# One-hot rows and columns of a token router, built for five token tiles by one comparison each, and their matmuls placed earlier

## The chip, the core and the metric

The kernel runs on one core of a Trainium2 chip. The metric is the device time of one execution in microseconds (us). Engines are named as in the profile: PE is TensorE (matmuls), PEld its weight loads, DVE is VectorE, ACT is ScalarE, POOL is GpSimd and SP is SyncE. Each engine works through a queue of its own in program order. What one engine hands to another is guarded by semaphores.

## The reference, cut to what matters

Attention through 32 packed vectors for each head (4 batches, 8 heads, 576 tokens), a mixture of 8 experts with the best two for each of the 2304 tokens, and a gated feed-forward layer:

```
p_packed = sm_attn(p, k, v);  x = sm_attn(q, p_packed, p_packed)
noisy = x @ w_gate + log1p(exp(x @ w_noise)) * noise
top2 of noisy for each token, weights by softmax over the two
out[token] += weight * (relu(x @ w1[e]) @ w2[e])      # for its two experts e
y = (silu(x @ w_gate2) * (x @ w_val)) @ w_out
```

The change is in the routing between the first two stages. Each pair (token, choice) gets a slot: expert number times 18 tiles of 128 rows, plus its rank in that expert. For the gathers of the experts' rows the kernel needs the inverse table `idx[row, column]`, which says what token sits in each slot. It is made by matmuls of one-hot matrices. For a tile of 128 tokens and choice k, `ohr[token, r] = (slot & 127 == r)` is 128 wide and `ohc[token, c] = (slot >> 7 == c)` is 144 wide (`NCOL`). The product of `ohr` transposed with `ohc` times the token number adds each token number into its place.

## The kernel before, in words

The whole program is one list of steps in the order in which it is issued. For attention, routing and the first two expert blocks that order stands in a string, `PLAN`, which is run step by step. `s1.t.h`, `mx`, `ex`, `et`, `eo`, `av`, `pp`, `pt`, `po`, `gp`, `s2`, `sa` to `sc`, `op` and `oo` are the steps of attention for group t of eight (scores, maximum, exponentials, transposes and so on). `u.i.f` is an up-projection of expert block i (12 matmuls 256 wide, written below as u), `h.i.f` splits its result into a high part `hh` (ACT, L664) and a low part `hl` (DVE, L665), and `d.i.f` is the down-projection (6 matmuls 512 wide). `g.i` gathers and transposes an expert block's rows (PE L610, then ACT L611 `xTh`, DVE L612 `xTl`). `L` turns the loader of expert weights: ACT makes the high part of a piece (L148), POOL or DVE the low part (L149).

`r.j` takes one step of the routing generator `route(j, ...)`. Router 0 and router 1 have five token tiles each and run inside attention; router 2 has ten tiles and runs beside the up- and down-projections of the first expert block. A step ends at each `yield`. Five tiles make a group; router 2 has two groups. A group's twelve steps are, before the change: ten steps of one pair (tile, choice) each, with two comparisons on DVE (L561 `ohr`, L563 `ohc`) and a scaling by the token number on ACT (L565 `ohv`); an eleventh with ten matmuls into one PSUM bank (L570); a twelfth in which DVE adds that bank to `idxf` (L573, at the end L579 into `idx`). Buffers: ten of `ohr`, three of `ohc`, ten of `ohv`.

The plan's steps around router 2's two groups, with the group's steps written as A1 to A12 and B1 to B12, stand so:

```
h.0.5 A1 A2 A3 d.0.4 A4 A5 A6 u.0.7 A7 A8 xo.7 d.0.5 A9 A10 h.0.6 g.1 A11
h.0.7 L A12 B1 B2 B3 B4 d.0.6 B5 u.1.0 B6 B7 B8 d.0.7 S u.1.1 B9 h.1.0 u.1.2
B10 u.1.3 B11 h.1.1 B12 d.1.0 (tail)
```

Router 0's group in the plan, cut: `oo.3.1`, steps 1 and 2, `s2.4.1`, steps 3 and 4, `mx.6.0 ... lg.1`, then `pp.5`, step 5, `pt.5`, step 6, `s1.6.1` (whose maximum is `mx.6.1`), step 7, and so on to step 12.

Of the kernel before, what the change touches and what calls it, by code (L numbers as in the profile page):

```python
# [14 lines left out]
F16 = mybir.dt.float16  # L15
I32 = mybir.dt.int32
U32 = mybir.dt.uint32
AF = mybir.ActivationFunctionType
ALU = mybir.AluOpType
# [10 lines left out]
NCOL = E * COLS  # L30
# [69 lines left out]
def body(ctx, tc, qT, kT, v, pT, noise, wgn, w1, w2, wx, out):  # L100
    nc = tc.nc
    ve = nc.vector
# [29 lines left out]
    def bank():  # L132
        return psum.tile([128, 512], F32, name="bank", tag="bank")
# [52 lines left out]
    ap2 = att.enter_context(tc.tile_pool(name="ap2", bufs=2, side="right"))  # L186
# [37 lines left out]
    def iota(name, shape, pattern, base=0, mult=0, dt=F32):  # L224
        t = ap1.tile(shape, dt, name=name)
        nc.gpsimd.iota(t, pattern=pattern, base=base, channel_multiplier=mult,
                       allow_small_or_imprecise_dtypes=True)
        return t
# [3 lines left out]
    io128 = iota("io128", [128, 128], [[1, 128]], dt=F16)  # L232
    io144 = iota("io144", [128, NCOL], [[1, NCOL]], dt=F16)
    tokid = iota("tokid", [128, NT], [[S, 4], [128, 5]], base=-MID, mult=1)
# [172 lines left out]
    def route(j, b0, b1):  # L407
        nt = 5 * (b1 - b0)
        t0 = 5 * b0
        l = lg[:, t0:t0 + nt, :]  # L410

        def tmp(name, dt=F32, shape=(128, nt, 8)):
            return ap1.tile(list(shape), dt, name=f"{name}_{j}")
        z = l[:, :, 8:16]
        nzb, fn, r, p, rz, u, den, s, w = (tmp(n) for n in ("nzb", "fn", "r", "p", "rz", "u", "den", "s", "w"))
# [104 lines left out]
        for c in range(nt):  # L520
            nc.tensor.matmul(rk[:, c + 1:], ones, mm[:, c:c + 1, :].to_broadcast([128, nt - c, 8]),
                             start=False, stop=c == nt - 1, skip_group_check=True)
# [20 lines left out]
        if b1 <= 2:  # L543
            s0 = tmp("s0", shape=(128, 2, 3))
            ve.scalar_tensor_tensor(s0, ixf[:, :, 0:3], float(FIRST - COLS * 128), sf[:, :, 0:3],
                                    op0=ALU.mult, op1=ALU.add)
# [6 lines left out]
        rf = tmp("rf", shape=(128, 2, 2, nt))  # L553
        ve.tensor_copy(rf, ri)
        yield
        for g in range(0, nt, 5):
            oh_ = []
            for c in range(g, g + 5):
                for k in range(2):
                    ohr = ap2.tile([128, 128], F16, name="ohr", bufs=10)  # L560
                    ve.tensor_scalar(ohr, io128, rf[:, 0, k, c:c + 1], None, op0=ALU.is_equal)  # L561
                    ohc = ap2.tile([128, NCOL], F16, name="ohc", bufs=3)
                    ve.tensor_scalar(ohc, io144, rf[:, 1, k, c:c + 1], None, op0=ALU.is_equal)  # L563
                    ohv = ap2.tile([128, NCOL], F16, name="ohv", bufs=10)
                    nc.scalar.activation(ohv, ohc, AF.Copy, scale=tokid[:, t0 + c:t0 + c + 1])  # L565
                    oh_.append((ohr, ohv))
                    yield
            pt = bank()[:, :NCOL]
            for n, (ohr, ohv) in enumerate(oh_):
                nc.tensor.matmul(pt, ohr, ohv, start=n == 0, stop=n == 9)  # L570
            yield
            if t0 + g + 5 < NT:
                ve.tensor_tensor(idxf, idxf, pt, op=ALU.add)  # L573
                if t0 + g + 5 == NT // 2:
                    for e in range(2):
                        ve.tensor_scalar(idx0[:, 2 * e:2 * e + 2], idxf[:, COLS * e:COLS * e + 2], float(2 * S - 1), None,
                                         op0=ALU.min)
            else:
                ve.tensor_tensor(idx, idxf, pt, op=ALU.add)  # L579
            yield  # L580
# [129 lines left out]

    loader = Loader([(*x[:3], engs[c]) for c, x in zip(ENG["lo"], [x for e in range(2) for x in expert_pieces(e, (ve, ve))])])
    jobs = [route(j, *x) for j, x in enumerate(JOBS)]
    blk_ = EARLY + [(0, 2, 3)]
    preps, UP, HID = {}, {}, {}
# [22 lines left out]
    def dn(i, f):  # L737
        down(*down_expert(blk_[i], f, HID.pop((i, f))))
    do = dict(wg=lambda: nc.sync.dma_start(wg, wgn), nz=lambda: nc.sync.dma_start(nz, noise), xo=store_x, lk=load_k, lv=load_v, lq=load_q, s1=s1, mx=max1, ex=exp1, et=e1t, eo=e1t_out, rc=rec1, av=av1, pp=pp,
              pt=ppt, po=ppt_out, gp=gproj, go=gproj_out, s2=s2, sa=s2a, se=s2e, sb=s2b, sc=s2c, op=oproj, oo=oout,  # L740
# [3 lines left out]
    for x in PLAN.split():  # L744
        x, _, n = x.partition("*")
# [416 lines left out]
    for i, blk in enumerate(blocks):  # L1162
        e, t0, nt = blk
# [191 lines left out]
```

## Time and profile before

| | |
|---|---|
| median of 3 runs | 1037.73 us (1034.54 to 1038.38) |
| profiled execution | 1037.31 us, span from first to last instruction 1035.5 us |
| mean granted clock of TensorE | 0.982 of full speed |
| PE busy | 978.0 us (94% of the span) |
| PEld, DVE, ACT, POOL busy | 864.9, 678.6, 421.5, 355.5 us |
| routing's comparisons on DVE (L561, L563) | 12.8 and 12.1 us, 40 instructions each, between 54.6 and 144 us |
| routing's ten-matmul groups on PE | four, ending at 73.4, 91.2, 133.2 and 144.7 us |

The profile is that of one execution. The 1.8 us between its time and its span lie around the program. A busy share is an average: DVE is busy for two thirds of the span as a whole, but almost without a gap in the attention and routing stage, which ends near 145 us; after it PE is busy nearly all the time.

### The profile page before, as it was taken

How to read it: one execution, taken by the hardware profiler on the slowest of the kernel's cores; microseconds unless marked ns; L12 is line 12 of the kernel's file. 1: busy time of each engine (PE TensorE's matmuls, PEld its weight loads, DVE VectorE, ACT ScalarE, POOL GpSimd, SP SyncE). 2: the span in 40 equal slices, each digit the busy share in tenths (PEclk: the TensorE clock that was granted, in tenths of full speed). 3: DMA queues.
4: the chain of work that ended last, by engine and by line, in shares of the span. 5: the costliest groups of instructions: out<-in, count | busy, mean ns of one | idle time of the engine just before them, and what ended most of it. 6: DMA issues, size and time to landing. Idle time of an engine off the chain costs nothing.

```text
span 1035.5 us, 15235 instructions
## 1 busy us (share of the span) xinstructions
PE 978.0 (94%) x5415; PEld 864.9 (84%) x5415; DVE 678.6 (66%) x1536; ACT 421.5 (41%) x859; POOL 355.5 (34%) x409
## 2 busy tenths in 40 slices
PE   6967799989999899998999999999999999999996
PEld 3534689979888798998988898999999999999995
DVE  5998973466565646555645475678865678756764
ACT  2665253465455545555544434222423224132220
POOL 1333532344643545445454414321232211111100
PEclk9978999999999999999999999999999999999999
DMA  8934543377675767666764679887798768777741
GB/s 288 299 122 146 170 136 116 126 273 269 212 264 191 270 204 251 229 202 245 246 225 159 194 210 311 238 236 214 217 303 235 230 184 255 234 199 222 216 147 65
DMA packets 99045, 221.41 MB, mean 214 GB/s; under 512 B 8080, under 2 KB 37392, under 8 KB 96656
## 3 DMA queue, kind: packets, MB, share of 16 engines
q0 software_dynamic: 46752, 104.87, 34.9%
q1 hardware_dynamic: 47024, 101.32, 28.9%
q10 hardware_dynamic: 5184, 14.16, 3.6%
q8 instruction: 45, 0.74, 0.3%
q14 instruction: 40, 0.33, 0.1%
HBM read 172.08 MB, written 48.23 MB: 213 GB/s over the span
## 4 chain that ended last, share of the span: by engine, by line
PE 74%; DVE 10%; DMA 5%; POOL 3%; issue 3%; ACT 3%; SPq 0%; ACTq 0%; POOLq 0%; DVEq 0%
PE bank L628 23%; PE bank L630 23%; PE bank L629 23%; DMA row<-x_dram,idx 3%; POOL sums L801 1%; DMA stg<-in_w 1%; PE bank L610 1%; PE bank L388 1%; POOL w L149 1%; DVE p L460 1%; DVE sums L824 1%; PE bank L919 1%; ACT w L148 1%; POOL sums L795 1%; DMA kt<-in_kT 1%
## 5 line engine op out<-in xcount | busy, mean ns | idle before, releaser
L628 PE MATMUL bank<-w 128*128 128x384 f32 x504 | 170.4, 338 | 0.6 <-ACT hh L993 0.5
L630 PE MATMUL bank<-w 128*128 128x384 f32 x504 | 168.7, 335 | 0.0
L629 PE MATMUL bank<-w 128*128 128x384 f32 x504 | 168.6, 334 | 0.0
L628 PE MATMUL bank<-xTh,w 128*128 128x256 f32 (+1 forms) x512 | 163.1, 319 | 2.8 <-DVE mt L787 2.8
L630 PE MATMUL bank<-xTh,w 128*128 128x256 f32 (+1 forms) x512 | 159.9, 312 | 0.0
L629 PE MATMUL bank<-xTl,w 128*128 128x256 f32 (+1 forms) x512 | 159.7, 312 | 0.0
L665 DVE SCALAR_TENSOR_TENSOR hl<-bank,hh 128x384 fp32r<-128x384 f32 (+1 forms) x128 | 62.4, 488 | 132.3 <-ACT hh L664 125.8
L871 POOL DMA_DIRECT2D w<-wq x72 | 54.4, 756 | 266.3 <-PE bank L630 266.3
L628 PE MATMUL bank<-w,hh 128*128 128x512 f32 x320 | 127.0, 397 | 6.1 <-ACT hh L664 6.1
L630 PE MATMUL bank<-w,hl 128*128 128x512 f32 x320 | 127.4, 398 | 2.8 <-DVE hl L665 2.8
L629 PE MATMUL bank<-w,hh 128*128 128x512 f32 x320 | 127.1, 397 | 0.0
L795 POOL TENSOR_TENSOR sums<-mt,ex 128x256 f32<-128x256 f32 x72 | 54.4, 755 | 170.4 <-DVE mt L787 163.8
L149 POOL TENSOR_TENSOR w<-stg,w 128x1024 fp32r<-128x1024 f32 x37 | 91.4, 2475 | 62.3 <-ACT w L148 62.0
L628 PEld LDWEIGHTS bank<-xTh,w 128*128 128x128 f32 x512 | 98.2, 192 | 7.8 <-DVE mt L787 3.5
L629 PEld LDWEIGHTS bank<-xTl,w 128*128 128x128 f32 x512 | 98.3, 192 | 3.5
L664 ACT ACTIVATE hh<-bank 128x384 fp32r<-128x384 f32 (+1 forms) x128 | 55.5, 433 | 111.5 <-PE bank L630 103.1
L630 PEld LDWEIGHTS bank<-xTh,w 128*128 128x128 f32 x512 | 98.2, 192 | 0.0
L628 PEld LDWEIGHTS bank<-w 128*128 128x128 f32 x504 | 94.6, 188 | 3.1 <-ACT hh L993 1.1
L629 PEld LDWEIGHTS bank<-w 128*128 128x128 f32 x504 | 94.7, 188 | 0.7
L630 PEld LDWEIGHTS bank<-w 128*128 128x128 f32 x504 | 94.6, 188 | 0.0
L630 PE MATMUL bank<-w,lg 128*128 128x512 f32 x204 | 79.7, 391 | 0.0
L629 PE MATMUL bank<-w,hg 128*128 128x512 f32 x204 | 79.7, 390 | 0.0
(222 smaller groups left out, 1838.4 us busy)
## 6 DMA issues: line engine op xcount, KB each, us to landing
w<-wq POOLq DMA_DIRECT2D x36, 1024.0 KB
stg<-in_w SPq DMA_DIRECT2D x64, 512.0 KB
w<-wq POOLq DMA_DIRECT2D x36, 768.0 KB
wd<-in_wx SPq DMA_DIRECT2D x72, 256.0 KB
w<-wxo POOLq DMA_DIRECT2D x18, 1024.0 KB
wq<-his ACTq DMA_DIRECT2D x24, 448.0 KB
wq<-sums SPq DMA_DIRECT2D x24, 448.0 KB
y_dram<-row SPq DMA_DIRECT2D x40, 256.0 KB
```

The lines of the kernel that those rows point to most:

```text
L148: nc.scalar.copy(hi, st)
L149: lo_eng.tensor_tensor(lo, st, hi.bitcast(F32), op=ALU.subtract)
L388: nc.tensor.matmul(PS["o", t, c][:n, :272], E2T[t][:, c * 128:c * 128 + n], PP[t], start=True, stop=True)
L460: el.scalar_tensor_tensor(p, p, c[k], x, op0=ALU.add, op1=ALU.mult)
L610: nc.tensor.transpose(ps[:, k, :n], src[:n, k * 128:(k + 1) * 128], ident[:n, :n])
L628: nc.tensor.matmul(ps, lh, rh, start=start, stop=False, skip_group_check=skip)
L629: nc.tensor.matmul(ps, lh, rl, start=False, stop=False, skip_group_check=skip)
L630: nc.tensor.matmul(ps, ll, rh, start=False, stop=stop, skip_group_check=skip)
L664: nc.scalar.activation(hh[:, :n], ps[:, :n], AF.Relu)
L665: ve.scalar_tensor_tensor(hl[:, :n], ps[:, :n], 0.0, hh[:, :n].bitcast(F32), op0=ALU.max, op1=ALU.subtract)
L795: nc.gpsimd.tensor_tensor(o, mf.rearrange("p (f n) -> p f n", f=2), ex.bitcast(F32).rearrange("p (f n) -> p f n", f=2), op=ALU.mult)
L871: nc.gpsimd.dma_start(w[:, :4 * m].rearrange("p (x n) -> p x n", x=4), src.rearrange("p h k n -> p (h k) n"))
```

## The change

Each group makes all ten `ohr` by one two-operand comparison (10 x 128 columns) and all ten `ohc` by another (10 x 144), with the iota row and the slot numbers both read through broadcast patterns. The iota rows are float16, the slot numbers float32. ACT scales `ohc` in place, once for each token tile (288 columns) instead of once for each pair. The first comparison is step 1 of the group, the second comparison and all five scalings are step 2, three steps are empty, the ten matmuls stand in step 6 (before: step 11), five steps are empty, and the addition stays in step 12. Both tiles have one buffer.

```diff
         for g in range(0, nt, 5):
-            oh_ = []
-            for c in range(g, g + 5):
-                for k in range(2):
-                    ohr = ap2.tile([128, 128], F16, name="ohr", bufs=10)
-                    ve.tensor_scalar(ohr, io128, rf[:, 0, k, c:c + 1], None, op0=ALU.is_equal)
-                    ohc = ap2.tile([128, NCOL], F16, name="ohc", bufs=3)
-                    ve.tensor_scalar(ohc, io144, rf[:, 1, k, c:c + 1], None, op0=ALU.is_equal)
-                    ohv = ap2.tile([128, NCOL], F16, name="ohv", bufs=10)
-                    nc.scalar.activation(ohv, ohc, AF.Copy, scale=tokid[:, t0 + c:t0 + c + 1])
-                    oh_.append((ohr, ohv))
-                    yield
+            ohr = ap2.tile([128, 5, 2, 128], F16, name="ohr", bufs=1)
+            ohc = ap2.tile([128, 5, 2, NCOL], F16, name="ohc", bufs=1)
+            at = [rf[:, x, :, g:g + 5].rearrange("p k c -> p c k").unsqueeze(3) for x in range(2)]
+            ve.tensor_tensor(ohr, io128[:, None, None, :].to_broadcast([128, 5, 2, 128]),
+                             at[0].to_broadcast([128, 5, 2, 128]), op=ALU.is_equal)
+            yield
+            ve.tensor_tensor(ohc, io144[:, None, None, :].to_broadcast([128, 5, 2, NCOL]),
+                             at[1].to_broadcast([128, 5, 2, NCOL]), op=ALU.is_equal)
+            for c in range(5):
+                nc.scalar.activation(ohc[:, c], ohc[:, c], AF.Copy, scale=tokid[:, t0 + g + c:t0 + g + c + 1])
+            yield
+            for _ in range(3):
+                yield
             pt = bank()[:, :NCOL]
-            for n, (ohr, ohv) in enumerate(oh_):
-                nc.tensor.matmul(pt, ohr, ohv, start=n == 0, stop=n == 9)
-            yield
+            for n in range(10):
+                nc.tensor.matmul(pt, ohr[:, n // 2, n % 2], ohc[:, n // 2, n % 2], start=n == 0, stop=n == 9)
+            for _ in range(6):
+                yield
             if t0 + g + 5 < NT:
                 ve.tensor_tensor(idxf, idxf, pt, op=ALU.add)
```

## Rows read from the trace of the kernel before

**Rows 1.** Windows: length, busy of PE, PEld, DVE, ACT, POOL; PE clock; DMA.

```profile
60.00:80.00 20.00, 13.54 (x77) 7.68 (x76) 19.25 (x76) 10.81 (x31) 8.12 (x5) 0.67 0.32 109
...
120.00:130.00 10.00, 6.97 (x44) 6.21 (x43) 9.77 (x44) 3.65 (x7) 4.66 (x2) 0.83 0.44 142
130.00:140.00 10.00, 10.00 (x73) 9.07 (x72) 9.20 (x36) 7.37 (x22) 2.40 (x1) 1.00 0.07 25
```

**Rows 2.** Waits of PE from 124 to 215 us: total, times, longest.

```profile
PE bank L519 <- DVE mm L516: 3.0, 1, 3.0
PE bank L570 <- ACT ohv L565: 2.0, 1, 2.0
```

**Rows 3.** Timeline of PE, router 2: start, duration, line, out<-in, [idle before <-releaser].

```profile
129.21 0.28 PE L628 MATMUL bank<-xTh,w 128*128 128x256 f32 x1
...
132.46 0.79 PE L570 MATMUL bank<-ohv,ohr 128*128 128x144 f16 x10
133.09 0.50 PE L628 MATMUL bank<-w,hh 128*128 128x512 f32 x1
...
136.01 0.40 PE L628 MATMUL bank<-w,hh 128*128 128x512 f32 x1
...
141.71 0.74 PE L570 MATMUL bank<-ohv,ohr 128*128 128x144 f16 x9
144.45 0.22 PE L570 MATMUL bank<-ohv,ohr 128*128 128x144 f16 x1 [2.00 <-ACT ohv L565]
```

**Rows 4.** Timeline of DVE in router 2, first and last of twenty comparisons, and what follows.

```profile
128.94 0.24 DVE L561 TENSOR_SCALAR ohr<-io,rf 128x128 f16<-128x128 f16 x1
...
132.06 0.26 DVE L563 TENSOR_SCALAR ohc<-io,rf 128x144 f16<-128x144 f16 x1
...
133.55 0.69 DVE L612 TENSOR_TENSOR xTl<-bank,xTh 128x512 fp32r<-128x512 f32 x1
134.16 0.41 DVE L665 SCALAR_TENSOR_TENSOR hl<-bank,hh 128x256 fp32r<-128x256 f32 x1
134.49 0.29 DVE L573 TENSOR_TENSOR idxf<-idxf,bank 128x144 f32<-128x144 f32 x1
...
134.86 2.41 DVE L563 TENSOR_SCALAR ohc<-io,rf 128x144 f16<-128x144 f16 x1
...
142.29 1.50 DVE L561 TENSOR_SCALAR ohr<-io,rf 128x128 f16<-128x128 f16 x1
```

**Rows 5.** Timeline of DVE: two-operand instructions from and to SBUF, two sizes.

```profile
103.24 1.20 DVE L149 TENSOR_TENSOR w<-stg,w 128x1024 fp32r<-128x1024 f32 x1
...
121.88 0.33 DVE L511 TENSOR_TENSOR oh<-io,expf 128x160 f32<-128x160 f32 x1
```

**Rows 6.** Timeline of ACT: four scalings, and SBUF-to-SBUF instructions of two widths.

```profile
55.04 1.40 ACT L565 ACTIVATE ohv<-ohc,tokid 128x144 f16<-128x144 f16 x4 [1.90 <-DVE ohc L563]
...
68.68 0.68 ACT L364 ACTIVATE s2a<-s2a 128x576 f32<-128x576 f32 x1 [1.22 <-POOL s2a L357]
...
94.44 0.44 ACT L364 ACTIVATE s2a<-s2a 128x288 f32<-128x288 f32 x1 [1.14 <-DVE s2a L357]
```

**Rows 7.** Timeline of POOL: a weight piece's low part.

```profile
134.81 2.40 POOL L149 TENSOR_TENSOR w<-stg,w 128x1024 fp32r<-128x1024 f32 x1 [8.06 <-ACT w L148]
```

**Rows 8.** Windows of one us after PE's stall that ends at 144.45.

```profile
145.00:146.00 1.00, 1.00 (x4) 0.73 (x3) 0.93 (x6) 0.00 (x0) 0.39 (x1) 0.50 0.95 373
...
148.00:149.00 1.00, 1.00 (x5) 0.80 (x4) 0.89 (x4) 0.24 (x2) 0.87 (x1) 0.82 0.77 209
```

**Rows 9.** Timelines of DVE and PE around router 0's group.

```profile
54.62 0.21 DVE L561 TENSOR_SCALAR ohr<-io,rf 128x128 f16<-128x128 f16 x1
...
57.84 0.33 PE L321 MATMUL bank<-ident,pp 128*128 128x128 f32 x1 [2.31 <-ACT pp L310]
...
60.98 0.45 DVE L269 TENSOR_REDUCE m<-bank 128x1 f32<-128x288 f32 x1
```

**Rows 10.** Waits of PE from 150 us to the end, the largest.

```profile
PE bank L610 <- DMA row<-x_dram,idx: 8.3, 4, 2.8
```

## The prediction

> **What bounds the kernel now.** I read the clock and the span first (one core, granted clock 0.982), then the windows. They show two regimes. Inside attention DVE is the full engine: from 60 to 80 us it is busy 19.25 of 20 us and PE only 13.5 [rows 1]. Beside the first expert block both are full: from 120 to 130 us DVE has 9.77 of 10, and from 130 to 140 PE has all 10 [rows 1]. In the second regime any wait of PE is paid in full by everything behind it. PE's waits from 124 us on are two: 3.0 us for DVE's `mm`, ahead of the one-hots and not touched here, and 2.0 us for the last scaling of router 2's second group [rows 2]. PE takes its instructions in order: nine of the ten matmuls ran at 141.71, the tenth at 144.45, and the down-projection behind it stood still [rows 3]. The last comparison but one had taken 1.50 us in place of 0.24 [rows 4]. After the wait the granted clock is 0.50, the lower of the two levels (1.2 GHz), in the window from 145 us and the two behind it, and 0.82 in the window from 148 [rows 8]: 3.0 + 0.36 us at half speed, so 1.7 us lost. The first group's matmuls, at 132.46, wait for nothing [rows 3].
>
> **What the edit costs on DVE and ACT.** Twenty comparisons of a group start from 128.94 to 132.06 without a gap, 3.12 / 19 = 0.164 us apart, so a group costs 3.28 us of DVE [rows 4]. One instruction on many columns is not in the trace. Two-operand instructions from SBUF take 0.33 us for 160 columns and 1.20 for 1024 [rows 5]: (1.20 - 0.33) / 864 = 1.01 ns a column. That gives 0.33 + 1120 x 1.01 ns = 1.46 us for 1280 columns and 1.62 us for 1440. A comparison lasts 0.24 but the next starts 0.16 after it, so consecutive ones overlap by 0.08: the pair ends 3.00 us after its start. DVE thus saves only 0.28 us a group, 1.1 in all four. Four scalings of 144 columns take 1.40 us, 0.35 each [rows 6]; 288 columns more cost 0.68 - 0.44 = 0.24 us, so 144 more cost 0.12, and one of 288 costs 0.47, five of them 2.35 us [rows 6]. ACT had room (7.37 of 10 us at its fullest here [rows 1]). What matters is that scaling, formerly running beside the comparisons, can now start only when the second big comparison is done: from the group's first comparison to its last scaled column 3.00 + 0.04 + 2.35 = 5.39 us, in place of 132.06 + 0.26 + 0.04 + 0.35 - 128.94 = 3.77 [rows 4, 6].
>
> [...]
>
> **What the move costs: router 2, first group.** The ten matmuls move from step 11 to step 6. In the plan's order, behind the group's first comparison PE has only `d.0.4` ahead of step 6, and it is through with it at 129.21, where `u.0.7` now starts [rows 3]. DVE starts the group at 128.94 [rows 4], ends at 131.94, and ACT at 131.98 + 2.35 = 134.33. PE would stand from 129.21 to 134.33: **5.1 us** of a stall that is not there today, since `u.0.7`, `d.0.5` and `g.1` (129.21 to 132.46, 3.25 us [rows 3]) were its cover and now queue behind it. The clock falls as after the 2.0 us wait: **1.7 us** more (0 to 1.7).
>
> **Second group.** DVE can't run ahead, because ahead of B1 it has the low part of `g.1`'s rows, and those wait for transposes that PE now does 3.25 us after the first group's matmuls. From the transposes' end: ACT's high part and hand-over about 0.65; then by the starts in [rows 4] 0.61 to `hl`, 0.33 to the addition, 0.21 to the first comparison (0.37 to the second one, less a pitch); then 5.39. Sum 7.2 us. PE has `d.0.6` and `u.1.0` meanwhile, 133.09 to 136.01, 2.92 us [rows 3]. The stall is 4.3 us. Between the two comparisons POOL wants its weight piece: ACT's cast of it follows `h.0.7`, so it comes while the first big comparison runs. Today that piece started at 134.81 and lasted 2.40 [rows 7], and the comparison that started behind it took 2.41 in place of 0.25 [rows 4]: DVE's SBUF comparisons and POOL's subtraction exclude each other, and POOL got in between two of them. Taken so again, +2.3: **6.6 us**; without, 4.3. Clock again **1.7**.
>
> **What goes away.** The 2.0 us wait and its 1.7 us of clock: d.1.0 has no matmuls of the router ahead of it. That is the change's gain, **3.7 us**.
>
> **Attention.** Router 0: ACT's first four scalings began at 55.04 and took 1.40, to 56.44 [rows 6]; now five end at 54.62 + 5.39 = 60.0. ACT's `pp.5` behind them, for which PE already waits 2.31 us at 57.84 [rows 9], comes 3.5 us later, then PE's transposes, the ten matmuls (0.6) and the scores whose maximum DVE took at 60.98 [rows 9]. By then DVE has work for part of it only; I put it 2.7 us late, and six later comparisons that are gone (1.0) give some back: +1.7. Bounds: -1 (DVE's saved instructions alone) and +3 (nothing given back). Router 1: its DVE has idle time at PE, so -0.2. I take **+1.5**. An extra PSUM bank held from step 6 to 12 I cost at nothing: the buffers are eight and few are live in router 2's stretch; if a bank is late, the like of it is the 2.0 us wait [rows 2], inside the range. Reading the bank, 0.29 us, is hidden as before [rows 4].
>
> **Sum.** 5.1 + 1.7 + 6.6 + 1.7 - 3.7 + 1.5 = 12.9 us. The later stages are bound by PE with buffers and gathers released by the program's own progress, so the delay passes on. The profiled execution took 1037.31 us (span 1035.5 and 1.8 around it), 0.4 below the median of the three runs: 1037.3 + 12.9 = **1050.2 us**.
>
> **Rivals.** Half a per cent (5.2 us) is about what a measurement of this kernel can tell from no change.
> *Two stalls, POOL not between* (0.22): if POOL's piece comes after both comparisons, -2.3: 1047.9. For it: the piece waits for a cast on ACT; against: 134.81 [rows 7].
> *Two columns a cycle* (0.05): the comparisons at half the price, 1.37 us less a group: stalls of 3.7 and 2.9 + 2.3, router 0 near +0.3; 3.7 + 1.7 + 5.2 + 1.7 - 3.7 + 0.3 = 8.9, 1046.2. Against it speaks [rows 5], one column in 1.01 ns. [...]
> *Absorbed later* (0.14): PE waits 8.3 us for gathered rows after 150 us, in four places [rows 10]. Were these DMAs on a clock of their own, a late PE would find them ready: 12.9 - 8.3 = 4.6, 1041.9, no measurable change. Against: POOL issues them behind its own work, which moves along.
> *Not slower* (0.09): PE reaches both sets of matmuls after the scaled columns, and the 3.7 us with DVE's 1.1 are pure gain: 1032.5. That needs DVE to begin the first group 5.1 us and the second 4.3 us earlier against PE than above. For it: DVE lost time at POOL's pieces shortly before, as in [rows 4]; against: PE waits on the same DVE queue just before, 3.0 us for `mm` [rows 2], so an earlier DVE makes PE earlier too.
>
> **Chances and range.** The forecast with both stalls and POOL between has 0.50, with its own range 1046.5 to 1053.5. Slower by over 0.5% takes the first three and a little of the fourth, 0.80; within, most of the last two, 0.16; faster, the not-slower case with more saved in attention, 0.04. Low bounds of the terms (stall 3.7, second 4.3, clock 0 and 1.7, attention -1) give 3.7 + 4.3 + 1.7 - 3.7 - 1 = 5.0 us, high ones (attention +3) 14.4; the range 1041 to 1053.5 leaves out about two in ten.
>
> **What would show it.** PE's waits: L570 on ACT's scaling twice in router 2, near 5 and 4 to 7 us, each followed by a granted clock of 0.50 for about 3 us; no wait at `d.1.0`; L561 at 1.46 and L563 at 1.62 us, or more beside POOL; ACT's scalings near 0.5. Wrong would be the forecast if the first group's wait were under 2 us, if DVE's timeline put B1 ahead of `g.1`'s rows, or if PE's waits after 150 us shrank by as much as the stalls add.

## The result, and the profile after

The changed kernel takes 1048.36 us (median of 6 runs, 1047.6 to 1052.54) against 1037.84 for the kernel before (6 runs, 1034.54 to 1042.45): a ratio of 1.0111, 95% interval 1.0081 to 1.0142. Its profiled execution took 1047.82 us, with a span of 1045.9 and a mean granted clock of 0.976. In this listing the lines behind the edit stand three lower than before: L572 is the router's ten matmuls, L631 to L633 the up- and down-projections, L566 the scaling.

The waits of PE between 124 and 215 us (waited for: total, times, longest) answer to [rows 2]:

```profile
PE bank L572 <- ACT ohc L566: 8.1, 2, 4.7
PE bank L519 <- DVE mm L516: 3.0, 1, 3.0
```

One wait of 2.0 us has become two that sum to 8.1, both for the scaled columns. PE's timeline shows where, and answers to [rows 3]:

```profile
130.68 0.40 PE L633 MATMUL bank<-w,hl 128*128 128x512 f32 x1
134.45 2.05 PE L572 MATMUL bank<-ohc,ohr 128*128 128x144 f16 x10 [3.37 <-ACT ohc L566]
136.25 0.56 PE L631 MATMUL bank<-xTh,w 128*128 128x256 f32 x1
...
143.95 0.28 PE L633 MATMUL bank<-xTh,w 128*128 128x256 f32 x1
148.94 2.10 PE L572 MATMUL bank<-ohc,ohr 128*128 128x144 f16 x10 [4.71 <-ACT ohc L566]
150.78 0.77 PE L631 MATMUL bank<-w,hh 128*128 128x512 f32 x1
...
157.72 0.40 PE L631 MATMUL bank<-w,hh 128*128 128x512 f32 x1
```

The wait in brackets is not the whole stall: the ten matmuls then come in pairs, each pair behind its own scaling, so that they spread over 2.05 us where they took 0.79 [rows 3]. From the end of `d.0.4` (131.08) to `u.0.7` (136.25) PE loses 5.17 us less the 0.65 of the matmuls themselves, 4.5; from the end of `u.1.0` (144.23) to `d.0.7` (150.78) 6.55 - 0.65 = 5.9. The last row is where `d.1.0` now runs with no wait ahead of it.

The producers, on DVE's timeline, answer to [rows 4]:

```profile
130.78 1.48 DVE L560 TENSOR_TENSOR ohr<-io,rf 128x1280 f16<-128x1280 f16 x1
132.18 1.65 DVE L563 TENSOR_TENSOR ohc<-io,rf 128x1440 f16<-128x1440 f16 x1
...
141.91 0.69 DVE L615 TENSOR_TENSOR xTl<-bank,xTh 128x512 fp32r<-128x512 f32 x1 [5.09 <-ACT xTh L614]
...
143.06 1.49 DVE L560 TENSOR_TENSOR ohr<-io,rf 128x1280 f16<-128x1280 f16 x1
144.47 3.80 DVE L563 TENSOR_TENSOR ohc<-io,rf 128x1440 f16<-128x1440 f16 x1
```

DVE, full before, now stands 5.09 us behind the transposes that PE does late: the first stall delays the second group. POOL's timeline has the piece that came between the two comparisons of that group, and ACT's has five scalings each of router 0's group and of router 2's second; they answer to [rows 7] and [rows 6]:

```profile
143.18 3.57 POOL L149 TENSOR_TENSOR w<-stg,w 128x1024 fp32r<-128x1024 f32 x1 [14.58 <-ACT w L148]
```

```profile
55.85 2.23 ACT L566 ACTIVATE ohc<-ohc,tokid 128x288 f16<-128x288 f16 x5 [4.35 <-DVE ohc L563]
57.99 0.92 ACT L253 COPY xs<-bank 128x272 f32<-128x272 f32 x3
58.81 1.27 ACT L310 ACTIVATE pp<-bank,sum 32x64 f32<-32x64 f32 x4
...
148.36 2.23 ACT L566 ACTIVATE ohc<-ohc,tokid 128x288 f16<-128x288 f16 x5 [5.26 <-DVE ohc L563]
```

The windows of one us behind both stalls (length, busy of PE, PEld, DVE, ACT, POOL, the granted clock, DMA) answer to [rows 8]. The clock is at the lower of the two levels that the trace shows, 0.50 of full speed, from near 136.2 to 139.6, and again from near 146.5, inside the second stall, to 153.3. At 0.50 a projection of 512 columns starts every 0.427 us (151.36 to 152.64, three of them), 1.20 columns a ns, which the forecast writes as 1.2 GHz; at 1.00 one starts every 0.230 us (139.74 to 140.43). The windows left out have 0.50 at 138 and from 147 to 151, and 1.00 from 140 to 146. Projections run through the last 2.5 us of the second stretch, from 150.78 on:

```profile
136.00:137.00 1.00, 0.86 (x6) 0.85 (x5) 0.42 (x1) 0.37 (x2) 0.00 (x0) 0.62 0.00 0
137.00:138.00 1.00, 1.00 (x7) 1.00 (x6) 0.00 (x0) 0.00 (x0) 0.00 (x0) 0.50 0.00 0
...
139.00:140.00 1.00, 1.00 (x5) 0.82 (x5) 0.00 (x0) 0.00 (x0) 0.00 (x0) 0.68 0.00 0
...
151.00:152.00 1.00, 1.00 (x4) 0.81 (x4) 0.00 (x0) 0.00 (x0) 0.00 (x0) 0.50 0.00 0
152.00:153.00 1.00, 1.00 (x3) 0.78 (x3) 0.55 (x1) 0.00 (x0) 0.00 (x0) 0.50 0.07 16
153.00:154.00 1.00, 1.00 (x7) 0.90 (x6) 0.14 (x1) 0.39 (x2) 0.00 (x0) 0.85 0.02 6
```

Around router 0 PE's timeline and DVE's answer to [rows 9]:

```profile
59.49 0.47 PE L321 MATMUL bank<-ident,pp 128*128 128x128 f32 x1 [5.78 <-ACT pp L310]
60.40 1.41 PE L572 MATMUL bank<-ohc,ohr 128*128 128x144 f16 x10
```

```profile
52.80 1.45 DVE L560 TENSOR_TENSOR ohr<-io,rf 128x1280 f16<-128x1280 f16 x1
...
58.95 0.24 DVE L403 TENSOR_TENSOR lg<-xs,xs 128x80 f32<-128x80 f32 x1 [1.22 <-ACT xs L253]
...
63.02 0.46 DVE L269 TENSOR_REDUCE m<-bank 128x1 f32<-128x288 f32 x1 [2.29 <-PE bank L263]
```

To see where the time went I cut each profiled execution at the same instructions: router 0's first comparison (A), its addition to `idxf` (B), router 1's addition (C), router 2's `mm` on DVE, L516 (D), the transposes of twelve rows on PE in `g.2` (E), and the end. In us:

| | start to A | A to B | B to C | C to D | D to E | E to end | span |
|---|---|---|---|---|---|---|---|
| before | 54.6 | 21.4 | 15.7 | 30.6 | 30.8 | 882.4 | 1035.5 |
| after | 52.8 | 24.7 | 15.4 | 31.2 | 40.7 | 881.1 | 1045.9 |
| difference | -1.8 | +3.4 | -0.3 | +0.6 | +9.9 | -1.3 | +10.4 |

Router 2's stretch (D to E) carries nearly all of it. The first column lies ahead of the first instruction that the change touches, and the last one scatters: in the eight kernels below it is 881.6 to 885.2.

### The profile page after: what moved, and what is told of

Its sections match the earlier page's. It is cut to its first block, busy times and chain, and to the rows that moved or that the text cites. A ratio compares the mean times of both kernels' runs of the same rounds, so it can differ in the third digit from the quotient of the medians.

```text
span 1045.9 us, 15139 instructions
## 1 busy us (share of the span) xinstructions
PE 982.2 (94%) x5415; PEld 868.2 (83%) x5415; DVE 675.3 (65%) x1464; ACT 417.0 (40%) x839; POOL 355.2 (34%) x409
## 4 chain that ended last, share of the span: by engine, by line
PE 71%; DVE 10%; DMA 6%; POOL 4%; ACT 4%; issue 3%; ACTq 0%; SPq 0%; POOLq 0%; DVEq 0%
PE bank L631 22%; PE bank L633 22%; PE bank L632 22%; DMA row<-x_dram,idx 3%; POOL sums L804 2%; DMA kt<-in_kT 1%; PE bank L613 1%; POOL w L149 1%; PE bank L388 1%; DMA stg<-in_w 1%; PE bank L263 1%; POOL sums L798 1%; DMA out<-row 1%; PE bank L922 1%; DVE sums L827 1%
## 5 line engine op out<-in xcount | busy, mean ns | idle before, releaser
L631 PE MATMUL bank<-w 128*128 128x384 f32 x504 | 170.8, 339 | 0.4 <-ACT hh L996 0.2
L633 PE MATMUL bank<-w 128*128 128x384 f32 x504 | 169.0, 335 | 0.0
L631 PE MATMUL bank<-xTh,w 128*128 128x256 f32 (+1 forms) x512 | 163.6, 320 | 2.8 <-DVE mt L790 2.8
L633 PE MATMUL bank<-xTh,w 128*128 128x256 f32 (+1 forms) x512 | 160.2, 313 | 0.0
L631 PE MATMUL bank<-w,hh 128*128 128x512 f32 x320 | 127.3, 398 | 5.7 <-ACT hh L667 5.7
L633 PE MATMUL bank<-w,hl 128*128 128x512 f32 x320 | 127.2, 398 | 2.1 <-DVE hl L668 2.0
L631 PEld LDWEIGHTS bank<-xTh,w 128*128 128x128 f32 x512 | 98.5, 192 | 7.6 <-DVE mt L790 3.4
L633 PEld LDWEIGHTS bank<-xTh,w 128*128 128x128 f32 x512 | 98.4, 192 | 0.0
L631 PEld LDWEIGHTS bank<-w 128*128 128x128 f32 x504 | 94.7, 188 | 3.1 <-ACT hh L996 1.0
L633 PEld LDWEIGHTS bank<-w 128*128 128x128 f32 x504 | 94.7, 188 | 0.0
L633 PE MATMUL bank<-w,lg 128*128 128x512 f32 x204 | 79.8, 391 | 0.0
```

The lines of the kernel that those rows point to most:

```text
L631: nc.tensor.matmul(ps, lh, rh, start=start, stop=False, skip_group_check=skip)
L633: nc.tensor.matmul(ps, ll, rh, start=False, stop=stop, skip_group_check=skip)
```

## Experiments

All eight kernels compute the whole reference. Their spans are cut as above; what is timed is given as a ratio to the kernel before, run beside them.

One thing differs among them ahead of the one-hots. In the kernel before, the change, "POOL's piece later", "columns first" with the matmuls in step 11 and the 16-bit kernel, POOL's weight piece runs beside `mm` of router 2, and PE waits 3.0 us for `mm`. In the other five `mm` is short and the piece holds the next large DVE instruction, L531 (2.5 us in place of 0.33); that wait is gone, and the one-hots come later against PE. DVE's timeline, kernel before and two pairs a step:

```profile
122.24 2.30 DVE L516 TENSOR_TENSOR mm<-oh 128x80 bf16<-128x80 f32 x1
```

```profile
120.54 0.24 DVE L516 TENSOR_TENSOR mm<-oh 128x80 bf16<-128x80 f32 x1
```

So a first group's wait can be compared only within one of these two sets; D to E holds the delay in either form. Why the piece falls differently was not traced.

**Matmuls back in step 11.** This keeps the big comparisons and lumped scalings and undoes the move alone.

```diff
-            for _ in range(3):
+            for _ in range(8):
                 yield
...
-            for _ in range(6):
-                yield
+            yield
```

> Big comparisons and scalings as in the changed kernel, but the ten matmuls back at step 11. Order theory (PE stands at matmuls placed ahead of their operands): in router 2's first group PE reaches them at the place of 132.46 while the scaling ends 5.3 us after the first comparison starts, so a wait of 1.8 us is left there (with up to 1.7 us of clock); none in the second group, and the old 2.0 us wait with its 1.7 us of clock is gone; attention costs 2 us more than before, since ACT's five scalings still stand ahead of pp.5. Sum near +1: 1036 to 1041 us. Rival, the batch theory (the big comparisons and lumped scalings cost the time wherever the matmuls stand): within 3 us of the changed kernel, 1045 to 1050.

Measured: 1042.56 us (10 runs), ratio 1.0047 (1.003 to 1.0064). PE's timeline of this kernel:

```profile
134.08 1.99 PE L572 MATMUL bank<-ohc,ohr 128*128 128x144 f16 x10 [1.88 <-ACT ohc L566]
...
144.67 0.92 PE L572 MATMUL bank<-ohc,ohr 128*128 128x144 f16 x10
146.79 0.50 PE L630 MATMUL bank<-w,hh 128*128 128x512 f32 x1 [1.20 <-ACT hh L666]
```

More than half of the loss goes with the move: D to E falls from 40.7 to 32.9. The second group waits for nothing at its matmuls. The time lies between the two expected ranges, above 1041 and below 1045, so the order alone does not explain all of it. As expected, the first group waits 1.88 us, and A to B is still 2.0 us longer than before, with five scalings in a block ahead of ACT's work for attention. Not expected: PE waits for ACT's `hh` behind the router's block, 3.0 us in two places. The granted clock did not fall here: it is 1.00 in every window of four us from 127 to 159. E to the end is 2.8 us longer than before, within the scatter of that column.

**Single comparisons, matmuls early.** The reverse: the code of before with two pairs a step, so that its matmuls too stand in step 6.

```diff
                     oh_.append((ohr, ohv))
-                    yield
+                yield
...
-            yield
+            for _ in range(6):
+                yield
```

> Single comparisons and scalings as in the kernel before, two pairs a step in steps 1 to 5, and the matmuls at step 6. Order theory: the last scaled column is there 3.8 us after the first comparison instead of 5.3, so PE waits near 3.5 us in router 2's first group and 3 to 5 in the second (with POOL's weight piece between comparisons), each with up to 1.7 us of clock, less the 3.7 us of before: +6 to +10, 1044 to 1048 us. Batch theory: nothing is batched, so as the kernel before, 1036 to 1040.

Measured: 1048.16 us (4 runs), ratio 1.0098 (1.0068 to 1.0128): the loss of the change without its comparisons. PE's timeline:

```profile
130.82 3.24 PE L570 MATMUL bank<-ohv,ohr 128*128 128x144 f16 x10 [3.78 <-DVE ohr L561]
...
143.56 3.18 PE L570 MATMUL bank<-ohv,ohr 128*128 128x144 f16 x10 [1.91 <-ACT ohv L565]
```

So the loss does not need the batched comparison. Both groups stall by the order alone; the batch makes the second stall worse (D to E 40.7 in place of 38.0) and the lumped scalings add to router 0.

**The change in router 2 alone.** Routers 0 and 1 keep single comparisons, one pair a step and matmuls in step 11.

```diff
+            if j == 2:
...
+            else:
+                for c in range(5):
+                    for k in range(2):
+                        ve.tensor_scalar(ohr[:, c, k], io128, rf[:, 0, k, g + c:g + c + 1], None, op0=ALU.is_equal)
+                        ve.tensor_scalar(ohc[:, c, k], io144, rf[:, 1, k, g + c:g + c + 1], None, op0=ALU.is_equal)
+                        nc.scalar.activation(ohc[:, c, k], ohc[:, c, k], AF.Copy, scale=tokid[:, t0 + g + c:t0 + g + c + 1])
+                        yield
...
```

> The change in router 2 alone; routers 0 and 1 keep single comparisons, a pair a step, matmuls at step 11 (their columns scaled in place). By the trace of the changed kernel router 2's stretch costs 9.7 us net and attention 3.7. Order theory: the attention part goes, the rest stays: 1044 to 1048 us, and router 0's group is back at the length of before. Rival (each of the four groups costs the same): half is left, 1042 to 1043.

Measured: 1047.11 us, ratio 1.0092 (1.0072 to 1.0113). A to B is back at 21.5, D to E stays at 41.9. PE's waits from 115 to 165 us:

```profile
PE bank L573 <- ACT ohc L567: 11.3, 2, 6.5
```

So router 2 alone makes the kernel slower by 0.9%. Of the 3.2 us that router 0 gets back, D to E takes 1.1 again, with two waits of 11.3 us in place of 8.1 (the 3.0 us for `mm` are gone, and the first group's wait is 6.5 in place of 3.4); the span is 2.0 below that of the change. Had each of the four groups cost the same, the time would have been 1042 to 1043, so that rival falls.

**POOL's piece later.** The plan turns `L` four of the router's steps later, behind B3, so that POOL's subtraction can't come between B1 and B2.

```diff
-... h.0.7 L r.2*5 d.0.6 r.2 u.1.0 ...
+... h.0.7 r.2*4 L r.2 d.0.6 r.2 u.1.0 ...
```

> The changed kernel with the loader's turn behind h.0.7 moved behind the second group's third step, so that ACT casts the weight piece after the five scalings. If POOL's subtraction held the second comparison (3.80 us instead of 1.65), that comparison takes 1.65, PE's wait in the second group falls by 2.1 us to near 2.6 by its first part, and the time by 2 us: 1046. If the long comparison has another cause it stays at 3.8 us and the time at 1048. A late piece could also make a later up-projection wait; the trace shows none within 10 us.

Measured: 1049.19 us, ratio 1.0113 (1.0092 to 1.0134), no gain over the change. DVE's timeline, and PE's:

```profile
142.02 1.48 DVE L560 TENSOR_TENSOR ohr<-io,rf 128x1280 f16<-128x1280 f16 x1
143.42 1.65 DVE L563 TENSOR_TENSOR ohc<-io,rf 128x1440 f16<-128x1440 f16 x1
```

```profile
145.75 2.10 PE L572 MATMUL bank<-ohc,ohr 128*128 128x144 f16 x10 [2.57 <-ACT ohc L566]
```

The mechanism is as expected: the comparison took 1.65 in place of 3.80, and the wait 2.57 in place of 4.71. The expected time is missed, since the clock took it back. Windows of one us of this kernel:

```profile
138.00:139.00 1.00, 1.00 (x4) 0.81 (x3) 0.00 (x0) 0.00 (x0) 0.00 (x0) 0.50 0.00 0
...
151.00:152.00 1.00, 1.00 (x6) 1.00 (x6) 0.38 (x1) 1.00 (x2) 0.06 (x1) 0.50 0.52 191
```

PE's projections run at a granted clock of 0.50 from 134.85 to 139.0 and from 147.60 to 152.3, 8.9 us; in the changed kernel from 136.4 to 139.6 and from 150.78 to 153.3, 5.7 us. Half of the difference is 1.6 us lost, an estimate by the granted clock, against 2.14 + 0.24 won at the two waits: D to E is 0.8 shorter. The other 1.3 us by which the span is longer lie in the rest of the program, which is within the scatter of the last column. Why the low level lasts longer here was not settled.

**Columns first, scalings spread, matmuls in step 11.** The columns' comparison, which has the longer follow-up, goes first; the scalings go one a step beside the rows' comparison.

```diff
-            ve.tensor_tensor(ohr, io128[:, None, None, :].to_broadcast([128, 5, 2, 128]),
-                             at[0].to_broadcast([128, 5, 2, 128]), op=ALU.is_equal)
-            yield
             ve.tensor_tensor(ohc, io144[:, None, None, :].to_broadcast([128, 5, 2, NCOL]),
                              at[1].to_broadcast([128, 5, 2, NCOL]), op=ALU.is_equal)
+            yield
+            ve.tensor_tensor(ohr, io128[:, None, None, :].to_broadcast([128, 5, 2, 128]),
+                             at[0].to_broadcast([128, 5, 2, 128]), op=ALU.is_equal)
             for c in range(5):
                 nc.scalar.activation(ohc[:, c], ohc[:, c], AF.Copy, scale=tokid[:, t0 + g + c:t0 + g + c + 1])
-            yield
-            for _ in range(3):
+                yield
+            for _ in range(4):
                 yield
...
-            for _ in range(6):
-                yield
+            yield
```

> Big comparisons, but the columns' one first, the scalings one a step in steps 2 to 6, and the matmuls back at step 11. Order theory: the last scaled column comes near 4.0 us after the group's first comparison starts (1.65 + 0.04 + 5 x 0.43, the rows' comparison done by then) instead of 5.3, and ACT's scalings no longer stand in one block ahead of pp.5. Router 0's group is back within 0.5 us of before (21.4 us from its first comparison to its addition); router 2's stretch loses the 2.0 us wait and its clock and keeps under 1 us of wait in the first group. 1033 to 1037 us, equal to before or up to 0.4% faster. Rival (big comparisons cost by themselves, since they hold DVE for 3 us): 1040 or more, as with the matmuls late alone.

Measured: 1035.25 us (12 runs, 1033.96 to 1036.47) against 1037.7 before (23 runs), ratio 0.9976 (0.9965 to 0.9987): faster than both kernels by a little. D to E is 28.25, 2.6 less than before, and A to B is 21.8. PE's waits from 124 to 165 us, and its timeline:

```profile
PE bank L519 <- DVE mm L516: 3.0, 1, 3.0
PE bank L630 <- ACT hh L666: 0.4, 1, 0.4
```

```profile
131.86 0.79 PE L572 MATMUL bank<-ohc,ohr 128*128 128x144 f16 x10
...
141.14 0.80 PE L572 MATMUL bank<-ohc,ohr 128*128 128x144 f16 x10
```

Neither group waits at its matmuls, although POOL came beside the second group's rows here too (DVE's timeline):

```profile
135.68 3.69 DVE L563 TENSOR_TENSOR ohr<-io,rf 128x1280 f16<-128x1280 f16 x1
```

**Columns first, matmuls left in step 6.** The exchange alone, scalings right behind the columns.

```diff
-            ve.tensor_tensor(ohr, io128[:, None, None, :].to_broadcast([128, 5, 2, 128]),
-                             at[0].to_broadcast([128, 5, 2, 128]), op=ALU.is_equal)
-            yield
             ve.tensor_tensor(ohc, io144[:, None, None, :].to_broadcast([128, 5, 2, NCOL]),
...
             yield
+            ve.tensor_tensor(ohr, io128[:, None, None, :].to_broadcast([128, 5, 2, 128]),
+                             at[0].to_broadcast([128, 5, 2, 128]), op=ALU.is_equal)
+            yield
             for _ in range(3):
```

> The changed kernel with the two big comparisons exchanged: columns and scalings first, rows second; matmuls stay at step 6. If PE waits for the chain comparison, then five scalings, each wait of router 2 falls by 1.4 us and router 0's group by near 1: 1044 to 1046. If it waits for DVE's two comparisons as a whole it stays at 1048.

Measured: 1046.2 us, ratio 1.0074 (1.0051 to 1.0097). A to B is 1.6 us shorter than in the change, D to E only 1.3. PE's waits from 124 to 165 us:

```profile
PE bank L572 <- ACT ohc L563: 6.0, 1, 6.0
PE bank L572 <- DVE ohr L565: 4.1, 1, 4.1
```

The second wait is now for the rows, whose comparison POOL held (3.64 us). The first is longer than the change's 3.4 us, since the 3.0 us for `mm` are gone ahead of it; the ten matmuls then take 1.38 us in each group, where the change's took 2.05 and 2.10. Router 2 is best compared with that of the kernel above that has the change there alone, which has no wait for `mm` either: D to E is 2.4 us shorter, 39.5 against 41.9. The exchange shortens the chain; it doesn't get it ahead of step 6.

**Two pairs a step, matmuls in step 11.** The code of before with every group's comparisons done sooner, to take away the old 2.0 us wait.

```diff
                     oh_.append((ohr, ohv))
-                    yield
+                yield
+            for _ in range(5):
+                yield
```

> The kernel before with two pairs a step in steps 1 to 5 and nothing else: single comparisons, matmuls at step 11. Order theory: all the gain that the change could have lies in the second group's 2.0 us wait with its clock, and that wait comes from two pairs of comparisons that stand in DVE's queue behind later work; with them issued early it goes: up to 3.7 us less, 1034 to 1037 us, and PE does not wait at L570. Rival (the wait comes from POOL's piece beside the comparison, 1.5 us in place of 0.24, wherever it stands): the wait and the time stay, 1037 to 1039.

Measured: 1038.69 us (12 runs), ratio 1.0001 (0.9983 to 1.0018), not the gain expected; D to E is 31.3, 0.5 more than before. PE's waits from 124 to 165 us, and its timeline:

```profile
PE bank L630 <- ACT hh L666: 1.8, 1, 1.8
PE bank L632 <- DVE hl L667: 1.2, 1, 1.2
```

```profile
129.21 2.48 PE L572 MATMUL bank<-ohv,ohr 128*128 128x144 f16 x10
...
140.38 0.80 PE L572 MATMUL bank<-ohv,ohr 128*128 128x144 f16 x10
...
145.81 0.50 PE L630 MATMUL bank<-w,hh 128*128 128x512 f32 x1 [1.81 <-ACT hh L666]
```

The wait at the second group's ten matmuls is gone, as expected, and PE waits at the down-projection instead, 1.81 us for `hh`. The granted clock falls behind that too: it is 0.55 from 146 to 148 us and 0.83 from 140 to 150, which is 1.7 us lost in those ten, as much as behind the old wait. ACT's `hh` is late there, since in ACT's queue it stands behind the router's tail, which waits for DVE (ACT's timeline):

```profile
145.27 0.22 ACT L602 ACTIVATE dt<-dt 128x20 f32<-128x20 f32 x1 [4.12 <-DVE dt L601]
145.39 0.64 ACT L666 ACTIVATE hh<-bank 128x256 fp32r<-128x256 f32 x2
```

The old wait had covered the next one. The 1.2 us for `hl` is no successor of it: it ends at 127.73, ahead of the first group, whose ten matmuls then spread over 2.48 us in place of 0.79, since the one-hots come later against PE here. Against these stand the 3.0 us that PE no longer waits for `mm`. So the trace shows `hh` in the place of the old wait, but the unchanged time is a sum of several shifts.

This kernel differs from "single comparisons, matmuls early" by the place of the matmuls alone, and in both `mm` is short. That makes the two the cleanest measure of the move: D to E 31.3 against 38.0, and ratios of 1.0001 against 1.0098.

**Slot numbers in 16 bits.** With float16 slot numbers every operand of the comparison is 16-bit.

```diff
-        rf = tmp("rf", shape=(128, 2, 2, nt))
+        rf = tmp("rf", F16, (128, 2, 2, nt))
```

> The changed kernel with the slot numbers held as float16, so that both operands of the comparisons are 16-bit. If two-operand instructions then go at two columns a cycle, 1280 columns take near 0.8 us and 1440 near 0.9, and PE's waits in router 2 fall by 1.4 us each. If the broadcast slot number (no step along the row) keeps them at one, 1.46 and 1.65 as before, and the time does not move.

Measured in one execution: 1052.4 us. DVE's timeline:

```profile
131.65 1.48 DVE L560 TENSOR_TENSOR ohr<-io,rf 128x1280 f16<-128x1280 f16 x1
133.04 1.65 DVE L563 TENSOR_TENSOR ohc<-io,rf 128x1440 f16<-128x1440 f16 x1
```

No instruction got shorter, and the time of the one execution is within the runs of the changed kernel (1047.6 to 1052.54). The 1280 columns of `ohr` took 1.48 us and the 1440 of `ohc` 1.65, with 16-bit operands as with the float32 slot numbers. The slot number is repeated along the row in both; whether that keeps the pace at this, no run shows.

## Why the prediction was right, and where its sizes were off

The forecast was 1050.2 us, 12.9 above the profiled execution of before; the profiled executions differ by 10.5. Its steps against the trace, in us:

| step | forecast | measured |
|---|---|---|
| comparison of rows, of columns | 1.46, 1.62 | 1.465, 1.648 |
| five scalings | 2.35 | 2.23 |
| stall in the first group | 5.1 | 4.5 |
| clock behind it | 1.7 | 0.38 + 0.50 + 0.50 + 0.32 = 1.7 |
| stall in the second group | 6.6 | 5.9 |
| clock behind it | 1.7 | 1.3 (from 150.78 on) |
| the old wait and its clock | -3.7 | gone |
| attention | +1.5 | +3.4 - 0.3 + 0.6 = +3.7 |

Router 2's terms as measured make 4.5 + 1.7 + 5.9 + 1.3 - 3.7 = 9.7; the stretch from D to E grew by 9.9.

**The mechanism is shown.** PE, in order, comes to the matmuls before the scaled columns exist: in the first group it is free at 131.08, and the first of them starts at 134.45. Undoing the move alone takes 7.8 us off that stretch; making the move with single comparisons puts 7.1 on it, 6.7 against the kernel that differs from it by the move alone; shortening the chain with the matmuls late leaves no wait at the matmuls. The rival that the change is not slower falls on the same rows, and that with two columns a cycle on the comparisons' durations, 1.465 and 1.648 us where it needed half of 1.46 and 1.62.

**POOL between the comparisons**, the step that set the forecast apart from its nearest rival, came: 3.80 us in place of 1.65. With the piece later the price went, so it is shown to be 2.14 at the wait, close to the 2.3 forecast. It is not worth that in time: taking it away gave nothing that could be measured. The measured time by itself would have fitted that rival better (1047.9); only the trace decides for the forecast's branch.

**Stalls a little too long.** In the first group PE came 1.7 us later than on the trace of before (the last matmul of `d.0.4` starts at 130.68 against 128.98), DVE 1.8 later (130.78 against 128.94), so this cancels. From the end of PE's last projection to the next one the two stalls are 5.17 and 6.55 us, against 5.1 and 6.6 forecast; the 0.65 of the ten matmuls' own work, which now runs between the scalings, is in both, and the forecast left it in.

**Attention was mis-sized**, 1.5 forecast, 3.7 measured, 3.4 of it in router 0. The direction was right: ACT's `pp.5` came late, and PE waited 5.78 us for it in place of 2.31 [rows 9]. The forecast priced the ten matmuls ahead of the scores at 0.6; they took 1.41. It gave back 1.0 for comparisons that are gone, but DVE could not use that: it waited 1.22 for `xs` behind the scalings and 2.29 for the scores, 3.5 together. The maximum of the scores came 10.2 us after the group's first comparison in place of 6.4, so 3.9 late where the forecast put 2.7; of the 1.0 given back, 0.5 came by B. The lumped scalings alone (big comparisons, matmuls late) cost 2.0 us in A to B, the early matmuls with two pairs a step 1.6, of which the two pairs make 0.5 by themselves; 2.0 + 1.6 is near the 3.4 of the change. The +0.6 from C to D is inside the scatter of that column, 30.3 to 31.2 in the eight kernels.

**What hid the miss.** The execution after began its first comparison 1.8 us sooner and ended 1.3 us shorter behind E. Neither was forecast. The first lies ahead of the change, and the second is inside the scatter between kernels; neither was traced to a cause. Router 2 came out 1.5 us below its forecast (9.9 for 11.4) and attention 2.2 above, so their misses nearly cancel. That the total was as close as 2.4 us is in part luck.

**Absorbed later** falls. PE's waits from 160 us on, the largest, answer to [rows 10]:

```profile
PE bank L613 <- DMA row<-x_dram,idx: 8.6, 4, 3.0
```

The gathers moved along with the program: 8.6 us against 8.3.

**The gain counted in full.** The forecast took 3.7 us off for the old wait. In the change nothing can tell whether it was there to be had, since the stalls ahead cover it; in the kernel with two pairs a step, taking that wait away gave nothing: `hh` was late next, with 1.8 us and 1.7 of clock. With columns first and the scalings spread, D to E is 2.6 shorter. The forecast named what is late next for the new stalls and not for this one.

## What to carry to other kernels

PE took its matmuls in the plan's order here, so move a consumer forward only to where its operands' chain has ended, counted from the producer's queue as it stands there; the waits of 3.37 and 4.71 us were paid by all that was queued behind them, and D to E grew by 9.9 us. The batch shortened the producer little (3.05 us a group in place of 3.28) and lengthened the time to its first result: the first scaling of router 2's first group began 3.09 us after the first comparison (130.78 to 133.87), where before it began 0.44 after (128.94 to 129.38). So put first the part with the longest follow-up and let that follow-up run beside the other part: with the matmuls in step 11, D to E was 28.25 that way and 32.9 without. And before counting a removed wait as a gain, look for the operand that is late next, as `hh` was here with 1.8 us.

## What the runs showed that was not expected

- A shorter wait was in part paid back by the clock: with POOL's piece later the two waits are 2.4 us shorter, and 3.2 us more of projections at the lower level cost an estimated 1.6 of it.
- POOL's subtraction and DVE's big comparisons held each other up in both directions here. The piece that began 0.12 us behind the first comparison took 3.57 us in place of 2.40 [rows 7]; the comparison behind both took 3.80 in place of 1.65.
- Lumping saved DVE next to nothing: 130.78 to 133.83 is 3.05 us a group against 3.28 [rows 4]. The medians of the two sizes, 1.465 us for 1280 columns and 1.648 for 1440, put a column at 1.14 ns, where the forecast had 1.01 from [rows 5]. Two large comparisons are worth 0.23 us a group over twenty small ones.
